# PV of two slots after fourteen rounds, in the MLP's groups of an attention and MLP block

## The chip, the cores and the metric

The kernel runs on one core of a Trainium2 chip. The metric is the device time of one execution in microseconds, and the numbers of a profile come from one profiled execution on that core. Engines are named as in the profile: PE is TensorE (PEld its weight loads), DVE is VectorE, ACT is ScalarE, POOL is GpSimd, SP issues the DMAs.

## The reference

The input x is 2048 tokens of 512 numbers. Its layer norm feeds two branches, which meet at the end:

```python
xn = _layernorm(x, axis=-1)
# A: qkv = xn @ wqkv; 32 heads of 16 numbers each
scores = jnp.einsum("bhqd,bhkd->bhqk", q, k) * (Dh ** -0.5)
p = _softmax(scores, axis=-1)
o = jnp.einsum("bhqk,bhkd->bhqd", p, v)
s = o.transpose(...).reshape(B, S, D) @ wo
# B: F = 1792
h = jnp.einsum("bsd,df->bsf", xn, w1) + b1
h = jnp.where(h > 0, h, 0) ** 2
g = _silu(jnp.einsum("bsf,fd->bsd", h, w2) + b2)
return x + s * g
```

Attention is over all 2048 x 2048 pairs of every head, so scores, exponentials and the product with v (PV) are the bulk of branch A. Branch B is a dense MLP.

## The kernel before

**Slots.** Attention is cut into 32 units (four heads by 512 queries), and each unit into 16 slots (128 keys each), 512 slots in all. A slot has four score matmuls (`exp_mm`, L1125: 128 keys by 512 queries, one for each head, contraction over 64 rows of the array), four exponentials on ACT (L1132) and, two slots later, four PV matmuls (`pv_mm`, L362), one for each head. A PV matmul uses all 128 rows and 32 of the columns of the array, so the four of a slot run side by side. The program has four of them in a slot; the profile lists each as two instructions, a first and a second pass.

**Maxima.** The softmax's shift is taken from the scores themselves, 24 slots ahead (`LEAD`): `max_mm` (L289) makes 128 queries by 512 keys of scores in a PSUM bank, and DVE reduces the bank to its row maxima (L296), four in each slot. When a unit's maxima are complete, `shift` transposes them on PE (L326) into a bank of the same pool, DVE splits them (L328, L329), `keep` writes them to DRAM (L335) and `back` brings them into the rows of the queries' tiles (L355). Steps put off with `later` (these two among them) run at the `begin` of the slot that is so many ahead.

**Banks.** PSUM's eight banks are given out as follows: three for scores that ACT reads (`pe`), three for scores that DVE reduces (`pm`), one for the MLP's sums (`pd`), one for PV's accumulation (`pv`; after a unit's sixteenth slot `evac`, L372, copies it out on ACT). Each pool hands its banks out in turn.

**Lanes and rounds.** Score, max and MLP matmuls contract over 64 rows, so that two of them run at once, one in each half (lane) of the array's rows. The program emits them in pairs, one in each lane; the text calls such a pair a round. All matmuls stand in one queue of PE, in the order in which the code emits them (the schedule is written by hand for all engines).

**Groups of the MLP.** `dense` yields the MLP's work. From the second of eight token chunks on (256 tokens each) most of it comes as blocks of four slots, which `long_slots` (L1207) runs: two halves, in each of which one lane has the MLP's twelve units (`D`) and the other has most of the scores. A half is written in two parts:

```python
for part, (mine, theirs) in enumerate((("D" * 10, "msmsmsmsms"), ("DDss", "mmsm"))):
```

`m` is a max matmul, `s` a score matmul. The ten rounds of the first part have five `m` and five `s` in the lane beside the MLP; the four of the second part have three `m` and three `s`. After each part stand `max_end` (DMAs of coming tiles), `shift_due` (a `shift` that is due) and PV of one slot: in a half's first part the slot two before the part's slot `st`, and so in its second. With PV between, a group is ten rounds, PV, four rounds, PV, ten rounds, PV, four rounds, PV.

There are two kinds of groups. In `first_pair` (w1, L508 and on) a unit is two matmuls of 256 columns, the sums go through a relu on ACT (L533), emitted in the second half's second part after its second round; chunks 1 to 7 have seven such groups each, 49 in all. In `second` (w2) a unit is one matmul of 512 columns; chunks 1 to 6 have six such groups each and chunk 7 has three, 39 in all. So there are 88 groups, or 176 halves. Other slots of the MLP (`slot`) have four `m`, four `s` and PV each.

**Tiles of exponentials.** `exp_mm` takes its output tile from a ring `pt`: 14 tiles, 17 from the second chunk on, when three staging tiles (`ex`) join, and 14 again at the end of the MLP. `oldest_first` turns the ring so that its oldest tile comes first whenever its length changes.

Of the kernel before, what the change touches and what calls it, by code (L numbers as in the profile page):

```python
# [8 lines left out]
F32 = mybir.dt.float32  # L9
# [7 lines left out]
P = 128  # L17
# [10 lines left out]
LEAD = 24  # L28
# [3 lines left out]
NPT = 14  # L32
# [7 lines left out]
def kernel(  # L40
# [55 lines left out]
    with ExitStack() as ph:  # L96
# [5 lines left out]
        pv = ph.enter_context(tc.tile_pool(name="pv", bufs=1, space=PSUM))  # L102

        rot = {}
        turn = {"ka": 0, "qm": 0, "qe": 0, "pt": 0}

        def ring(name):
            t = rot[name][turn[name] % len(rot[name])]
            turn[name] += 1
            return t  # L110

        def oldest_first(name):
            n = turn[name] % len(rot[name])
            rot[name] = rot[name][n:] + rot[name][:n]
            turn[name] = 0

        def make_ring(name, pool, numbers, width):
            rot.setdefault(name, []).extend(
# [201 lines left out]
        def shift_due(g):  # L320
            if late and late[0][0] <= g:
                shift(late.pop(0)[1])
# [91 lines left out]
        def mlp_tasks(mp):  # L414
# [3 lines left out]
            ex = mp.enter_context(tc.tile_pool(name="ex", bufs=1))  # L418
# [123 lines left out]
            def second(c, tt):  # L542
                hT = state["hT"]
                ps = pd.tile([P, D], F32, name="pd_t")
                u = up.tile([P, D], F32, name="u")
                th = rs[tt].rearrange("p a b -> p (a b)")
                ts_ = slice(tt * P, (tt + 1) * P)

                if c == 0 and tt == 0:
                    for k in range(5, FO):  # L550
                        later(k - 4, lambda k=k: load_w2(k, 2))

                def post():
                    nc.scalar.activation(u, ps, AF.Copy)  # L554
                    nc.gpsimd.tensor_tensor(u, u, b2_t, op=ALU.add)  # L555
                    later(2, gate)

                def gate():

                    nc.scalar.activation(th, u, AF.Tanh, scale=0.5)  # L560
                    nc.gpsimd.tensor_scalar(th, th, 0.5, 0.5, op0=ALU.mult, op1=ALU.add)
                    nc.gpsimd.tensor_tensor(u, u, th, op=ALU.mult)
                    t0 = c * CW + tt * P
                    later(4, lambda: nc.sync.dma_start(g_d[t0 : t0 + P, :], u))

                mms = terms3(ps, [
                    (lambda a, q, fo=fo: hT[q, a, fo, ts_], lambda b, q, fo=fo: w2t[q, b, fo])
                    for fo in range(FO)
                ])
                if c == 0:  # L570
                    yield from halves(mms, (6,) * 7, post, 1)
                    return
                if c == NCK - 1 and tt:

                    for i, task in enumerate(halves(mms, (6,) * 7, post, 1)):
                        if i == 4:
                            oldest_first("pt")
                            rot["pt"][:] = [t for t in rot["pt"] if all(t is not x for x in rot["ex"])]
                        yield task
                    return  # L580

                if tt:
                    yield from halves(mms[:6], (6,), None, 1)
                    mms = mms[6:]
                for k in range(0, 36, 12):
                    yield from block(mms[k : k + 12], 1, post if tt and k == 24 else None)
                if not tt:
                    yield from halves(mms[36:], (6,), post, 1)
# [10 lines left out]
                yield [], None  # L599
            for c in range(NCK):  # L600
                if c == 1:

                    oldest_first("pt")
                    rot["pt"][:0] = rot["ex"]
                if c == 0:
                    for fo in range(FO):
                        yield from first(c, fo)
                else:
                    for f in range(FO // 2):
                        yield from first_pair(c, f)  # L610
                if c + 1 < NCK:
                    load_xc(c + 1)
                    state["part"] = 0
                    for k in range(8):
                        later(13 + k, load_part)
                else:
                    m1.close()
                    wo_setup()
                for tt in range(CW // P):
                    yield from second(c, tt)  # L620
# [246 lines left out]
        st = right(ln, "wq_st", 1)  # L867
# [217 lines left out]
        for g in range(LEAD):  # L1085
            shift_due(g)
            for j in range(2):
                max_mm(g, j)
            pump(8)
            for j in range(2):  # L1090
                max_mm(g, j)
            pump(8)
            max_end(g)
            if g == 0:
                raw_r = [load_w("wv", 3 * P, ((D + P, 3 * P),))]
            if g == 3:
                for ko in range(KO):
                    split_w(wr_t, ko, slice(3 * P, 6 * P), raw_r[0][:, ko])
                ln.close()
                pools["v"] = ph.enter_context(tc.tile_pool(name="vp", bufs=1))  # L1100
            if g == 12:
                s1.close()
                ep = ph.enter_context(tc.tile_pool(name="ep", bufs=1))
                rot["pt"] = [ep.tile([P, 512], F32, name=f"pt{i}") for i in range(NPT)]
                pools["n"] = ph.enter_context(tc.tile_pool(name="np", bufs=1))
            if g == 16:
                load_v(0)
                nc.sync.dma_start(b1_t, b1.rearrange("(fo p) -> p fo", p=P), allow_slow_non_contiguous=True)
                nc.sync.dma_start(b2_t, b2[None, :].to_broadcast([P, D]))
            if g % 2 and g < 16:  # L1110
                c, i = divmod(g // 2, 2)
                nc.sync.dma_start(
                    xn_d[i, :, :, c * 512 : (c + 1) * 512], xTs[c][:, i].bitcast(F32)
                )
        first.close()

        def exp_mm(st, j, pts, spare):
            u, kb = divmod(st, 16)
            qd = u // 4
            b = 64 * (j % 2)  # L1120
            if spare:
                se = pm.tile([P, 512], F32, name="pm_t")
            else:
                se = pe.tile([P, 512], F32, name="se")
            nc.tensor.matmul(  # L1125
                se, kas[qd, j // 2][b : b + 64, kb * P : (kb + 1) * P],
                qes[u][j // 2][b : b + 64, :],
                start=True, stop=True,
            )
            pts[j] = ring("pt")  # L1130
            assert all(t is not pts[j] for d in pts_all.values() if d is not pts for t in d.values()), (st, j)
            return nc.scalar.activation(pts[j], se, AF.Exp, scale=0.25)  # L1132

        pos = {}
# [1 line left out]
        def pv_step(st, pts):  # L1136
            u, kb = divmod(st, 16)
            if kb == 0:
                pos[0] = pv.tile([P, 512], F32, name="po")
            pv_mm(pos[0], u // 4, kb, pts)  # L1140
            if kb == NT - 1:
                if u < NU - 2:
                    evac(pos[0], u)
                elif u == NU - 2:
                    unit_inner(pos[0])
                else:
                    unit_final(pos[0])
# [19 lines left out]
                yield from wo_last(c)  # L1167

        pts = {}
        pts_all = pts  # L1170

        def slot(st, mms, post, fill=0):
            g = st + LEAD
# [33 lines left out]
        def long_slots(st0, units, post):  # L1207
# [11 lines left out]
            for h in range(2):  # L1219
                own, other = units[h], 1 - h  # L1220
                for part, (mine, theirs) in enumerate((("D" * 10, "msmsmsmsms"), ("DDss", "mmsm"))):
                    st = st0 + 2 * h + part
                    if st > st0:
                        begin(st)
                    for i, ops in enumerate(zip(mine, theirs)):
                        for lane in (h, other) if part else (other, h):
                            o = ops[0] if lane == h else ops[1]
                            if o == "D":
                                own.pop(0)()
                            elif o == "m":  # L1230
                                max_mm(g0, lane)
                            else:
                                use = s(lane)
                                if part and lane == h and i == 2:
                                    last_use[0] = use
                        if part and h and i == 1 and post is not None:
                            post()
                    max_end(st + LEAD)
                    shift_due(st + 1 + LEAD)
                    pv_step(st - 2, pts.pop(st - 2))  # L1240
            if post is not None:
                last_use[0] = None
            assert not todo[0] and not todo[1] and not units[0] and not units[1]
# [82 lines left out]
```

## Time and profile before

| | us |
|---|---|
| median of two runs | 1686.23 |
| the two runs | 1684.71, 1687.75 |
| span of the profiled execution | 1684.0 |
| PE busy | 1655.3 |
| DVE busy | 1349.0 |
| ACT busy | 1192.2 |
| POOL busy | 525.5 |

The span is from the first to the last instruction of the one profiled execution; it lies 0.7 below the faster of the two runs and 2.2 below their median, and that execution's own time is not listed apart from its span. In a row of the timeline stand the start and the length in microseconds, then engine, line, operation, output and inputs, shapes, and how many instructions the row merges; a bracket tells how long the engine was idle before and what ended that. Matmuls are pipelined, so their records overlap: the time from one start to the next tells more than a record's length.

### The profile page before, as it was taken

What the parts mean: (1) busy time and instruction counts of PE and PEld (TensorE: products, weight loads), DVE (VectorE), ACT (ScalarE), POOL (GpSimd) and SP (SyncE); (2) the same over time, 40 slices, a digit from 0 to 9 for tenths busy, and PEclk for the clock granted to TensorE, in tenths of its full rate; (3) what the DMA queues carried; (4) which work ended last, traced back from release to release, by engine and by line L of the source; (5) the groups of instructions that cost most, each with busy time, mean ns of one, the idle gap of its engine ahead of it and who ended that gap; (6) DMA issues with size and microseconds to landing.
All of it is one profiled execution on the core that took longest, in us unless ns stands there. A gap on an engine that the chain in (4) does not pass through costs nothing.

```text
span 1684.0 us, 35391 instructions
## 1 busy us (share of the span) xinstructions
PE 1655.3 (98%) x13296; PEld 941.3 (56%) x13296; DVE 1349.0 (80%) x2296; ACT 1192.2 (71%) x2354; POOL 525.5 (31%) x544
## 2 busy tenths in 40 slices
PE   6999999999999999999999999999999999999998
PEld 5766565556545655565466456545655565555533
DVE  6255688888888888888888888888888888887632
ACT  7211477777777777777777777777777777776685
POOL 4335566522212321231133113311221233134333
PEclk9999999999999999999999999999999999999998
DMA  8648566434333333433333334323433352157444
GB/s 282 177 144 268 165 204 186 117 83 141 90 90 92 116 83 99 100 105 78 103 117 85 85 93 142 95 65 105 137 81 83 82 151 57 44 169 228 140 125 134
DMA packets 156723, 208.00 MB, mean 124 GB/s; under 512 B 51272, under 2 KB 71240, under 8 KB 155016
## 3 DMA queue, kind: packets, MB, share of 16 engines
q1 hardware_dynamic: 156552, 205.74, 42.2%
q8 instruction: 105, 1.72, 0.4%
q14 instruction: 66, 0.54, 0.1%
HBM read 149.30 MB, written 56.09 MB: 122 GB/s over the span
## 4 chain that ended last, share of the span: by engine, by line
PE 88%; issue 4%; DMA 3%; POOL 2%; SPq 1%; DVE 1%; ACT 0%; POOLq 0%; ACTq 0%
PE po L362 27%; PE pm_t L289 17%; PE pd_t L236 16%; PE se L1125 12%; PE pd_t L204 6%; PE se L916 5%; PE se L947 3%; POOL ts L740 1%; POOL ts L741 1%; DMA oc<-on_d 0%; PE pm_t L816 0%; PE pm_t L326 0%; DMA xt<-in_A_x_dram 0%; DMA xc<-xn_d 0%; DMA hl<-r_d 0%
## 5 line engine op out<-in xcount | busy, mean ns | idle before, releaser
L296 DVE TENSOR_REDUCE mx<-pm_t 128x1 f32<-128x512 f32 x2048 | 1275.2, 684 | 233.0 <-PE pm_t L289 139.7
L1132 ACT ACTIVATE pt<-se 128x512 f32<-128x512 f32 x1730 | 902.9, 611 | 254.7 <-PE se L1125 221.6
L289 PE MATMUL pm_t<-ka,qm 64*128 64x512 f32 x2048 | 797.1, 423 | 3.9 <-DVE mx L296 3.7
L1125 PE MATMUL se<-qe,ka 64*128 64x512 f32 x2000 | 685.9, 402 | 0.0
L362 PE MATMUL po<-pt,v 128*32 128x512 f32 x3556 | 544.3, 604 | 0.0
L289 PEld LDWEIGHTS pm_t<-ka,qm 64*128 64x128 f32 x2048 | 352.8, 184 | 279.5 <-DVE mx L296 252.2
L1125 PEld LDWEIGHTS se<-qe,ka 64*128 64x128 f32 x2000 | 339.5, 184 | 21.3 <-issue 5.5
L236 PEld LDWEIGHTS pd_t<-xc,w1s 64*128 64x128 f32 x2352 | 292.1, 187 | 82.3 <-issue 82.2
L236 PE MATMUL pd_t<-xc,w1s 64*128 64x256 f32 x2352 | 332.2, 288 | 0.0
L236 PE MATMUL pd_t<-w2t,hT 64*128 64x512 f32 x936 | 259.9, 410 | 0.0
L236 PEld LDWEIGHTS pd_t<-w2t,hT 64*128 64x128 f32 x936 | 156.0, 184 | 71.2 <-issue 65.4
L362 PE MATMUL po<-ex,v 128*32 128x512 f32 x540 | 192.3, 605 | 0.0
L1132 ACT ACTIVATE ex<-se 128x512 f32<-128x512 f32 x270 | 147.5, 614 | 36.6 <-PE se L1125 31.6
L536 POOL TENSOR_TENSOR r<-r 128x512 f32<-128x512 f32 x49 | 50.9, 1040 | 331.3 <-ACT r L533 331.3
L362 PEld LDWEIGHTS po<-pt,v 128*32 128x32 f32 x3556 | 79.9, 108 | 132.3 <-issue 111.6
L555 POOL TENSOR_TENSOR u<-u,b_t 128x512 f32<-128x512 f32 x16 | 20.5, 1284 | 307.5 <-ACT u L554 307.5
L204 PE MATMUL pd_t<-w2t,hT 64*128 64x512 f32 x408 | 105.6, 391 | 0.0
L400 POOL TENSOR_TENSOR ot<-ot,hl 128x512 f32<-128x512 f32 x31 | 39.8, 1284 | 185.5 <-DMA hl<-r_d 134.8
L204 PE MATMUL pd_t<-wot,oc 64*128 64x512 f32 x336 | 90.4, 405 | 2.4 <-DVE m L316 0.8
L204 PEld LDWEIGHTS pd_t<-wot,oc 64*128 64x128 f32 x336 | 58.6, 184 | 49.1 <-DVE mx L296 12.5
L204 PEld LDWEIGHTS pd_t<-w2t,hT 64*128 64x128 f32 x408 | 72.6, 184 | 8.9
L533 ACT ACTIVATE r<-pd_t,b_t 128x256 f32<-128x256 f32 x98 | 41.1, 470 | 50.1 <-PE pd_t L236 50.1
(111 smaller groups left out, 1110.4 us busy)
## 6 DMA issues: line engine op xcount, KB each, us to landing
w1s<-w_d SPq DMA_DIRECT2D x196, 256.0 KB
qm<-q_d SPq DMA_DIRECT2D x384, 32.0 KB
qe<-q_d SPq DMA_DIRECT2D x384, 32.0 KB
ka<-k_d SPq DMA_DIRECT2D x96, 128.0 KB
xn_d<-xT SPq DMA_DIRECT2D x8, 1024.0 KB
k_d<-hl SPq DMA_DIRECT2D x32, 256.0 KB
q_d<-hl SPq DMA_DIRECT2D x32, 256.0 KB
xc<-xn_d SPq DMA_DIRECT2D x16, 512.0 KB
```

The lines of the kernel that those rows point to most:

```text
L204: mm = nc.tensor.matmul(out_, lh(r), rh(r), start=first_ and lane == 0, stop=last_ and lane == 1, skip_group_check=True,)
L236: mm = nc.tensor.matmul(out_, lh(r), rh(r), start=first_ and lane == 0, stop=last_ and lane == 1, skip_group_check=True,)
L289: nc.tensor.matmul(ps, qms[u][p][64 * j : 64 * j + 64, qb * P : (qb + 1) * P], kas[qd, p][64 * j : 64 * j + 64, kc * 512 : (kc + 1) * 512] ...
L296: return nc.vector.tensor_reduce(mxs[u][:, c, kc : kc + 1], ps, axis=AX.X, op=ALU.max)
L362: nc.tensor.matmul(po[32 * j : 32 * j + 32, :], vs[qd][:, (4 * kb + j) * VW : (4 * kb + j) * VW + 32], pts[j], start=(kb == 0), stop=(kb = ...
L400: nc.gpsimd.tensor_tensor(ot, ot, hl[:, 1].bitcast(F32), op=ALU.mult)
L533: nc.scalar.activation(r[:, i], ps[:, i * CW : (i + 1) * CW], AF.Relu, bias=b1_t[:, fo : fo + 1])
L536: nc.gpsimd.tensor_tensor(r, r, r, op=ALU.mult)
L916: nc.tensor.matmul(out_, lh(slice(0, P)), rh(slice(0, P)), start=first_, stop=last_)
L947: nc.tensor.matmul(out_, lh(slice(0, P)), rh(slice(0, P)), start=first_, stop=last_)
L1125: nc.tensor.matmul(se, kas[qd, j // 2][b : b + 64, kb * P : (kb + 1) * P], qes[u][j // 2][b : b + 64, :], start=True, stop=True,)
L1132: return nc.scalar.activation(pts[j], se, AF.Exp, scale=0.25)
```

## The change

In `long_slots` a half is no longer cut by PV after its first part. After all fourteen rounds comes `shift_due`, and then PV of two slots in one go. `begin` and `max_end` stay between the parts, and the order of `m`, `s` and `D` stays.

The exponentials' tiles no longer come from a ring but from a list of free tiles: `exp_mm` takes the first, and `pv_step` appends a slot's four tiles when its PV is emitted. The three staging tiles are put at the head of the list at the second chunk, and are kept out of it from the end of the MLP on (`gone_pt`).

```diff
@@ exp_mm
-            pts[j] = ring("pt")
+            pts[j] = free_pt.pop(0)
@@ pv_step
             pv_mm(pos[0], u // 4, kb, pts)
+            free_pt.extend(t for _, t in sorted(pts.items()) if all(t is not x for x in gone_pt))
@@ mlp_tasks
-                    oldest_first("pt")
-                    rot["pt"][:0] = rot["ex"]
+                    free_pt[:0] = rot["ex"]
@@ long_slots
                     max_end(st + LEAD)
-                    shift_due(st + 1 + LEAD)
-                    pv_step(st - 2, pts.pop(st - 2))
+                shift_due(st + 1 + LEAD)
+                for kb in (st - 3, st - 2):
+                    pv_step(kb, pts.pop(kb))
```

Lines move up by two to four in the changed kernel: the max matmul is L287 there, its reduction L294, the score matmul L1121, PV L360, the transpose L324.

More of the change, by code (lines that the diff above doesn't have):

```diff
@@ L104 @@
         rot = {}
-        turn = {"ka": 0, "qm": 0, "qe": 0, "pt": 0}
+        turn = {"ka": 0, "qm": 0, "qe": 0}
         def ring(name):
@@ L110, in ring @@
             return t
[L112 to L115, printed above, removed]
+        free_pt = []
+        gone_pt = []
         def make_ring(name, pool, numbers, width):
@@ L576, in second @@
                         if i == 4:
-                            oldest_first("pt")
-                            rot["pt"][:] = [t for t in rot["pt"] if all(t is not x for x in rot["ex"])]
+                            gone_pt.extend(rot["ex"])
+                            free_pt[:] = [t for t in free_pt if all(t is not x for x in gone_pt)]
                         yield task
@@ L601, in mlp_tasks @@
                 if c == 1:
-                    oldest_first("pt")
-                    rot["pt"][:0] = rot["ex"]
+                    free_pt[:0] = rot["ex"]
                 if c == 0:
@@ L1103 @@
                 ep = ph.enter_context(tc.tile_pool(name="ep", bufs=1))
-                rot["pt"] = [ep.tile([P, 512], F32, name=f"pt{i}") for i in range(NPT)]
+                free_pt.extend(ep.tile([P, 512], F32, name=f"pt{i}") for i in range(NPT))
                 pools["n"] = ph.enter_context(tc.tile_pool(name="np", bufs=1))
@@ L1129, in exp_mm @@
             )
-            pts[j] = ring("pt")
-            assert all(t is not pts[j] for d in pts_all.values() if d is not pts for t in d.values()), (st, j)
+            pts[j] = free_pt.pop(0)
             return nc.scalar.activation(pts[j], se, AF.Exp, scale=0.25)
@@ L1169 @@
         pts = {}
-        pts_all = pts
         def slot(st, mms, post, fill=0):
```

## Prediction

> **What bounds the kernel now.** I read the page first, then busy times by stretch, then the timeline of single groups, engine by engine.
>
> ```profile
> span 1684.0 us, 35391 instructions
> ...
> PE 1655.3 (98%) x13296; PEld 941.3 (56%) x13296; DVE 1349.0 (80%) x2296; ACT 1192.2 (71%) x2354; POOL 525.5 (31%) x544
> ```
>
> PE is busy for 98% of the span: PE is the bound, and DVE at 80% is the next. The change touches only groups of the MLP, so I look at what a half of such a group does there: the first row below is a half of the first kind (w1), the second a half of the second kind (w2).
>
> ```profile
> 907.55:913.26 5.71, 5.71 (x61) 3.54 (x57) 4.97 (x9) 4.30 (x10) 1.68 (x3) 1.00 0.30 52
> 924.65:930.30 5.65, 5.65 (x48) 2.79 (x44) 4.97 (x9) 4.58 (x11) 2.59 (x3) 1.00 0.75 234
> ```
>
> The columns are length, then PE, PEld, DVE, ACT and POOL busy, then the clock, granted in full (1.00). PE does not rest in either. DVE has 4.97 of 5.71 in a half: 0.7 us is all the slack it has. So I need to know where in a half the slack lies. The timeline of PE in the first of these halves (an L289 row is an `m`, an L1125 row an `s`, L362 is PV), then DVE and ACT in the same half:
>
> ```profile
> 907.55 0.50 PE L289 MATMUL pm_t<-ka,qm 64*128 64x512 f32 x1
> ...
> 909.53 0.40 PE L289 MATMUL pm_t<-ka,qm 64*128 64x512 f32 x1
> ...
> 909.77 0.39 PE L1125 MATMUL se<-qe,ka 64*128 64x512 f32 x1
> ...
> 910.14 1.06 PE L362 MATMUL po<-pt,v 128*32 128x512 f32 x8
> ...
> 911.14 0.50 PE L289 MATMUL pm_t<-ka,qm 64*128 64x512 f32 x1
> ...
> 911.48 0.39 PE L289 MATMUL pm_t<-ka,qm 64*128 64x512 f32 x1
> ...
> 911.94 0.39 PE L289 MATMUL pm_t<-ka,qm 64*128 64x512 f32 x1
> ...
> 912.26 1.06 PE L362 MATMUL po<-pt,v 128*32 128x512 f32 x8
> 913.26 0.50 PE L289 MATMUL pm_t<-ka,qm 64*128 64x512 f32 x1
> ```
>
> ```profile
> 908.09 3.08 DVE L296 TENSOR_REDUCE mx<-pm_t 128x1 f32<-128x512 f32 x5 [0.21 <-PE pm_t L289]
> 911.71 1.89 DVE L296 TENSOR_REDUCE mx<-pm_t 128x1 f32<-128x512 f32 x3 [0.54 <-PE pd_t L236]
> ```
>
> ```profile
> 908.39 2.56 ACT L1132 ACTIVATE pt<-se 128x512 f32<-128x512 f32 x5 [0.39 <-PE pd_t L236]
> 911.97 0.84 ACT L533 ACTIVATE r<-pd_t,b_t 128x256 f32<-128x256 f32 x2 [1.03 <-PE pd_t L236]
> ```
>
> Rounds follow each other by 0.24 (909.53 to 909.77). Five `m` come in the first part; DVE takes their five banks in one run of 3.08, one each 0.60 ((3.08 - 1.89) / 2), and gets through it just as PV ends. The PV that is taken out here is the pause in which DVE catches up.
>
> **The change part by part.**
>
> *PV taken out between the parts: a gain.* The tenth round starts at 909.77 and the eleventh at 911.14: 1.37 in place of 0.24. The round after it comes 0.34 later (911.48), again not 0.24. So one PV costs 1.13 + 0.10 = 1.23. It is not removed but put behind another PV, and there it needs no change between row lanes and column tiles. At the end of the kernel PVs follow each other directly:
>
> ```profile
> 1666.30 1.04 PE L362 MATMUL po<-pt,v 128*32 128x512 f32 x8
> ```
>
> Two passes of four take 1.04 from the first start to the last end there. A pass after another lasts 0.59, and the four start within 0.02, so one pass follows the other by 1.04 - 0.59 - 0.02 = 0.43; the 0.59 stands in the tile's own row:
>
> ```profile
> L362 PE MATMUL po<-pt,v x3556: 592/593/618, 195.4 to 1668.3; 128*32 128x512 f32 x198
> ```
>
> A PV behind a PV costs 0.86, so each half gains 1.23 - 0.86 = 0.37. With 176 halves (49 + 39 groups of two) that is 65 us, if nothing takes its place.
>
> The Trainium skill, "TensorEngine Tiling (Array Packing)", Tiling Modes, says that changing the tiling mode drains the TensorE. The trace agrees, at 0.37 for a change there and back. By that rule alone the sum would end at 1684 - 65 = 1619.
>
> *The eighth max of a half: a wait that is new.* Without PV, the fourteenth round, which has the half's eighth `m`, would start 2.22 + 4 x 0.235 = 3.16 after the half's first `m`. But `pm` has three banks, so the eighth `m` needs the bank of the fifth, and DVE has to be through with five reductions. The first starts 0.54 after its matmul (907.55 to 908.09), five take 3.08: 3.62. DVE reads these five back to back already now, so nothing brings that end forward. How a PE that stood still for a bank goes on is seen in the few slots without MLP work:
>
> ```profile
> 1486.91 0.49 PE L289 MATMUL pm_t<-ka,qm 64*128 64x512 f32 x1 [0.32 <-DVE mx L296]
> ...
> 1487.33 1.07 PE L362 MATMUL po<-pt,v 128*32 128x512 f32 x8
> ...
> 1489.61 0.50 PE L289 MATMUL pm_t<-ka,qm 64*128 64x512 f32 x1 [0.31 <-DVE mx L296]
> ...
> 1490.04 1.07 PE L362 MATMUL po<-pt,v 128*32 128x512 f32 x8
> ```
>
> ```profile
> 1486.16 2.48 DVE L296 TENSOR_REDUCE mx<-pm_t 128x1 f32<-128x512 f32 x4 [0.38 <-PE se L1125]
> ```
>
> The first of those four reductions ends at 1486.16 + 0.69 = 1486.85, and the matmul starts 0.06 later. From it to PV are 0.42 and 0.43, where a half without a wait has 0.32 (911.94 to 912.26): after a wait the weights are still to be loaded. So the eighth `m` starts at 3.62 + 0.06 = 3.68, PV at 3.68 + 0.42 = 4.10. The first PV takes 1.00 to the next matmul (912.26 to 913.26), the second 0.86 more, so the next half starts at 5.96. The seventh `m` waits too (for the fourth reduction, 3.02 + 0.06 = 3.08), but its two rounds more, 0.34 + 0.23, end at 3.65 and are covered by the eighth's wait.
>
> A half now takes 5.71 or 5.65, and then 5.96 in both kinds, since nothing of the MLP's rounds is in that chain any more: 98 halves x 0.25 = 24.5, and 78 x 0.31 = 24.2. Together 49 us lost, with the gain of 65 already in it. DVE then finishes eight reductions at 0.54 + 3.08 + 3 x 0.60 = 5.42 and sits idle until 5.96 + 0.54: the two PVs in a row are longer than what three banks hold for it.
>
> The Trainium skill, "TensorEngine Tiling (Array Packing)", PSUM Bottleneck, warns that tiling speeds up the TensorE but not the emptying of PSUM, which may become the bottleneck. It gives no price, but it speaks against this change, and the reductions' rows bear it out at 0.60 each. By it the kernel ends at 1733 instead of 1619 before the rest is counted.
>
> *The eighth score of a half: a wait that costs nothing.* ACT's three banks tie the eighth `s` to the fifth exponential: 908.39 - 907.55 = 0.84, plus 2.56, is 3.40, plus 0.06 is 3.46. It hides behind the eighth `m` at 3.68. Without that cover it would still hold the half to 3.46 + 0.42 + 1.86 = 5.74. The relus of the first kind (0.84) stand behind the fifth exponential on ACT, so they delay only the last three, whose banks are asked for after PV.
>
> *`shift` after the second part: a small loss.* One of 16 slots has it, 22 of the 352.
>
> ```profile
> 901.64 0.50 PE L289 MATMUL pm_t<-ka,qm 64*128 64x512 f32 x1
> ...
> 904.22 0.28 PE L326 MATMUL pm_t<-ident,m 128*16 128x128 f32 x1
> 904.43 1.07 PE L362 MATMUL po<-pt,v 128*32 128x512 f32 x8
> ```
>
> That half takes 5.91 (901.64 to 907.55), 0.20 more than its neighbour. Moved, the transpose needs the bank of the sixth `m`, free at 3.62 + 0.60 + 0.06 = 4.28; PV follows 0.21 to 0.31 later, at 4.49 to 4.59 instead of 4.10. That is 0.39 to 0.49 in place of 0.20: 22 x 0.24 = 5 us. Its DVE work (two short operations) falls into DVE's idle time. `keep` and `back` go to SP one slot later, in the tenth and eleventh of a unit's slots, and their rows are read from slot 16 of that count: over four slots, some 11 us, lie between, against 0.6 us for an issue of `keep`:
>
> ```profile
> L335 SPq DMA_DIRECT2D sh_d<-sh x64: 608/618/755, 159.5 to 1615.9; - x64
> ```
>
> *The free list, `begin`, `evac`: nothing.* Sixteen tiles of exponentials are held at most, of 17. In the second half an exponential writes a tile that PV has just read, but its score matmul stands behind that PV in PE's queue, so the wait for it covers the other. With fewer than 16 tiles it would not fit at all. `begin` issues the same DMAs at the same places. `evac` has fourteen rounds instead of ten before PV asks for its bank, and the MLP's sums have one PV more for their relu.
>
> Sum, against the profiled span: 1684 + 49 + 5 = 1738. The median of the two runs lies 2 above that span: 1740.
>
> **The rivals.**
>
> *It pays off (faster).* If the eighth `m` finds its bank free, a half takes 5.34, and the time is 1686 - 65 = 1621. It decides at a wait of zero, so at five reductions within 3.16 - 0.54 - 0.06 = 2.56; the row says 3.08, and also ACT's 3.46 would have to go. It is also what the page's rule on drains would give by itself. Only a bank count that I read wrong brings it. Chance 7%.
>
> *The wait costs less (within 2%).* If PE has the weights of the eighth `m` loaded by the time of its bank, because that last wait is short (3.65 to 3.68), PV follows 0.32 later and a half takes 5.86: 98 x 0.15 + 78 x 0.21 = 31, with no more for `shift`: 1686 + 31 = 1717. Should only ACT's wait hold (5.74), it is 98 x 0.03 + 78 x 0.09 = 10: 1696. Against it: in both rows with a wait PV came at 0.42 and later. Chance 18%.
>
> *It costs more.* If each of the two waits adds its reload of 0.10 (the seventh's isn't covered), a half takes 6.06: 98 x 0.35 + 78 x 0.41 = 66, and with 5 for `shift` 1757. Chance 15%, in the slow class with the forecast.
>
> **How the numbers follow.** Forecast 60%, costs more 15%, costs less 18%, pays off 7%. The time is the forecast's, 1740. The range goes from 1716 (the cheap wait) to 1757; outside lie the 7%, the ACT case and a little above, less than 2 in 10. Two per cent, about what a measurement of this kernel can tell from no change, is 34 us: 1720. Faster by over 2%: 0.07. Within 2%: 0.18. Slower by over 2%: 0.75.
>
> **What would show it.** In the changed kernel, halves of both kinds repeat every 5.96; the eighth max starts 3.68 after the first, right after the end of a reduction, and PV 0.42 after it, lasting 1.9 in one row of 16. DVE has eight reductions in one run of about 4.9 and then 1.0 idle, in place of 0.5 and 0.2. Weight loads of the max matmul idle longer for DVE. The forecast is wrong if the eighth `m` starts near 3.2, if halves stay near 5.3, or if the two kinds of halves differ as they do now.

## The result, and the profile after

| | before | after |
|---|---|---|
| median of two runs, us | 1686.23 | 1736.57 |
| span of the profiled execution, us | 1684.0 | 1736.0 |

The changed kernel takes 1.030 of the time (95% interval 1.027 to 1.033): 50 us more, where 54 were forecast (1740).

First the page of the kernel after: busy times, and the chain that ended last.

```profile
PE 1703.8 (98%) x13296; PEld 1023.9 (59%) x13296; DVE 1332.8 (77%) x2296; ACT 1196.5 (69%) x2354; POOL 525.2 (30%) x544
...
PE 85%; DVE 6%; issue 3%; DMA 2%; POOL 2%; SPq 1%; ACT 0%; POOLq 0%; DVEq 0%; ACTq 0%
PE po L360 25%; PE pm_t L287 21%; PE pd_t L234 12%; PE se L1121 11%; PE pd_t L202 6%; DVE mx L294 5%; PE se L912 5%; PE se L943 3%; DMA xt<-in_A_x_dram 1%; DMA g<-g_d 1%; POOL ts L737 1%; POOL ts L736 1%; PE pm_t L812 0%; PE pm_t L324 0%; SPq L132 0%
```

The chain of the kernel before, from its page:

```profile
PE 88%; issue 4%; DMA 3%; POOL 2%; SPq 1%; DVE 1%; ACT 0%; POOLq 0%; ACTq 0%
PE po L362 27%; PE pm_t L289 17%; PE pd_t L236 16%; PE se L1125 12%; PE pd_t L204 6%; PE se L916 5%; PE se L947 3%; POOL ts L740 1%; POOL ts L741 1%; DMA oc<-on_d 0%; PE pm_t L816 0%; PE pm_t L326 0%; DMA xt<-in_A_x_dram 0%; DMA xc<-xn_d 0%; DMA hl<-r_d 0%
```

PE is still busy for 98%, so by busy shares nothing seems to wait. The chain tells otherwise: the reductions (mx L294) now have 5% of it, where the list before doesn't name them. Next, the timeline of PE in one half of the first kind (L287 is an `m`, L360 PV), and DVE's:

```profile
940.77 0.49 PE L287 MATMUL pm_t<-ka,qm 64*128 64x512 f32 x1
...
943.25 0.50 PE L287 MATMUL pm_t<-ka,qm 64*128 64x512 f32 x1
...
943.84 0.50 PE L287 MATMUL pm_t<-ka,qm 64*128 64x512 f32 x1
...
944.44 0.49 PE L287 MATMUL pm_t<-ka,qm 64*128 64x512 f32 x1
944.86 0.62 PE L360 MATMUL po<-ex,v 128*32 128x512 f32 x1
...
946.72 0.49 PE L287 MATMUL pm_t<-ka,qm 64*128 64x512 f32 x1
```

```profile
941.30 4.88 DVE L294 TENSOR_REDUCE mx<-pm_t 128x1 f32<-128x512 f32 x8 [1.08 <-PE pd_t L234]
947.25 3.08 DVE L294 TENSOR_REDUCE mx<-pm_t 128x1 f32<-128x512 f32 x5 [1.07 <-PE pm_t L287]
```

The last three `m` of the half (sixth to eighth) start 2.48, 3.07 and 3.67 after the first, 0.60 apart: DVE's pace, not PE's 0.24. PV follows the eighth by 0.42, and the next half starts at 5.95. DVE has its eight reductions in one run and then 1.07 idle. The second row below is a half of the second kind (w2); the columns are length, then PE, PEld, DVE, ACT and POOL busy, then the clock.

```profile
940.77:946.72 5.95, 5.95 (x62) 4.00 (x58) 4.88 (x8) 4.13 (x8) 1.29 (x1) 1.00 0.05 9
970.00:975.95 5.95, 5.95 (x52) 3.18 (x44) 4.95 (x9) 4.13 (x8) 0.00 (x1) 1.00 0.27 66
```

Both kinds take 5.95, where they had 5.71 and 5.65. PE counts as busy in all of it: a matmul's record is 0.39 to 0.50 long and overlaps the next, so a wait of 0.35 (from the sixth `m` to the seventh 0.59 pass in place of 0.24) disappears in it. The views of waits say as little. Two rows of the lists of waits, before and after (weight loads, what they waited for, us in total, times, the longest):

```profile
PEld pm_t L289 <- DVE mx L296: 252.2, 352, 1.6
```

```profile
PEld pm_t L287 <- DVE mx L294: 255.0, 436, 1.4
```

### The profile page after: what moved, and what is told of

Read it like the earlier page. It is cut to its first block, busy times and chain, and to the rows that moved or that the text cites. A ratio compares the mean times of both kernels' runs of the same rounds, so it can differ in the third digit from the quotient of the medians.

```text
span 1736.0 us, 35235 instructions
## 1 busy us (share of the span) xinstructions
PE 1703.8 (98%) x13296; PEld 1023.9 (59%) x13296; DVE 1332.8 (77%) x2296; ACT 1196.5 (69%) x2354; POOL 525.2 (30%) x544
## 4 chain that ended last, share of the span: by engine, by line
PE 85%; DVE 6%; issue 3%; DMA 2%; POOL 2%; SPq 1%; ACT 0%; POOLq 0%; DVEq 0%; ACTq 0%
PE po L360 25%; PE pm_t L287 21%; PE pd_t L234 12%; PE se L1121 11%; PE pd_t L202 6%; DVE mx L294 5%; PE se L912 5%; PE se L943 3%; DMA xt<-in_A_x_dram 1%; DMA g<-g_d 1%; POOL ts L737 1%; POOL ts L736 1%; PE pm_t L812 0%; PE pm_t L324 0%; SPq L132 0%
## 5 line engine op out<-in xcount | busy, mean ns | idle before, releaser
L294 DVE TENSOR_REDUCE mx<-pm_t 128x1 f32<-128x512 f32 x2048 | 1259.2, 683 | 299.1 <-PE pm_t L287 195.9
L287 PE MATMUL pm_t<-ka,qm 64*128 64x512 f32 x2048 | 862.1, 441 | 3.9 <-DVE mx L294 3.6
L1121 PE MATMUL se<-qe,ka 64*128 64x512 f32 x2000 | 718.1, 418 | 0.0
L287 PEld LDWEIGHTS pm_t<-ka,qm 64*128 64x128 f32 x2048 | 365.2, 184 | 348.6 <-DVE mx L294 255.0
L360 PE MATMUL po<-pt,v 128*32 128x512 f32 x3544 | 508.2, 600 | 0.0
L1121 PEld LDWEIGHTS se<-qe,ka 64*128 64x128 f32 x2000 | 353.1, 185 | 18.1 <-issue 5.5
L234 PE MATMUL pd_t<-xc,w1s 64*128 64x256 f32 x2352 | 306.5, 284 | 0.0
L234 PE MATMUL pd_t<-w2t,hT 64*128 64x512 f32 x936 | 239.3, 401 | 0.0
L360 PE MATMUL po<-ex,v 128*32 128x512 f32 x552 | 223.0, 599 | 0.0
L1127 ACT ACTIVATE ex<-se 128x512 f32<-128x512 f32 x276 | 164.5, 605 | 51.2 <-PE pd_t L234 34.0
L360 PEld LDWEIGHTS po<-pt,v 128*32 128x32 f32 x3544 | 97.4, 108 | 164.6 <-issue 152.9
L202 PE MATMUL pd_t<-w2t,hT 64*128 64x512 f32 x408 | 105.8, 392 | 0.0
L81 POOL TENSOR_TENSOR hT<-r,hT 128x512 fp32r<-128x512 f32 x56 | 72.2, 1288 | 4.7
```

The source lines that it names most:

```text
L81: (lo or nc.gpsimd).tensor_tensor(dst[1], raw, dst[0].bitcast(F32), op=ALU.subtract)
L202: mm = nc.tensor.matmul(out_, lh(r), rh(r), start=first_ and lane == 0, stop=last_ and lane == 1, skip_group_check=True,)
L234: mm = nc.tensor.matmul(out_, lh(r), rh(r), start=first_ and lane == 0, stop=last_ and lane == 1, skip_group_check=True,)
L287: nc.tensor.matmul(ps, qms[u][p][64 * j : 64 * j + 64, qb * P : (qb + 1) * P], kas[qd, p][64 * j : 64 * j + 64, kc * 512 : (kc + 1) * 512] ...
L294: return nc.vector.tensor_reduce(mxs[u][:, c, kc : kc + 1], ps, axis=AX.X, op=ALU.max)
L360: nc.tensor.matmul(po[32 * j : 32 * j + 32, :], vs[qd][:, (4 * kb + j) * VW : (4 * kb + j) * VW + 32], pts[j], start=(kb == 0), stop=(kb = ...
```

## The experiments

The theory under test is the bank theory: a half is lengthened by its eighth max, which waits until DVE has emptied the bank of the fifth. Rivals are the list of free tiles, ACT's banks, the two PVs in a row, and DVE's total load.

| run | median, us | against the kernel before (95% interval) |
|---|---|---|
| e1_list_only | 1685.96 | 0.9999 (0.9989 to 1.0008) |
| e2_thin_max | 1682.24 | 0.9972 (0.9962 to 0.9981) |
| e3_thin_exp | 1736.28 | 1.0300 (1.0282 to 1.0319) |
| e4_thin_both | 1626.81 | 0.9655 (0.9636 to 0.9675) |
| e5_before_thin_both | 1684.92 | 0.9993 (0.9984 to 1.0003) |
| e6_second_half | 1709.57 | 1.0142 (1.0124 to 1.0159) |
| e7_two_banks | 1941.43 | one run |
| e8_thin_max_scores_first | 1646.09 | 0.9757 (0.9742 to 0.9771) |
| e9_scores_first | 1778.68 | 1.0541 (1.0523 to 1.0558) |

**The list alone.**

```diff
                     max_end(st + LEAD)
-                shift_due(st + 1 + LEAD)
-                for kb in (st - 3, st - 2):
-                    pv_step(kb, pts.pop(kb))
+                    shift_due(st + 1 + LEAD)
+                    pv_step(st - 2, pts.pop(st - 2))
```

> The changed kernel with PV back where it was (ten rounds, PV of one slot, four rounds, PV of one slot, shift after either part); only the list of free tiles stays. Bank theory (the loss is the eighth max waiting for one of three banks that DVE reduces): the list costs nothing, halves take 5.70 and 5.65 as before, 1686 us in all, within 3 us of the kernel before. List theory (tiles taken in another order make exponentials wait for PV): a good part of the 50 us stays, 1700 to 1736.

1685.96: the list of free tiles costs nothing. All of the 50 us belongs to the place of PV and of `shift`, which moved with it.

**Thin reductions.** `thin[0]` is set inside `long_slots` alone.

```diff
-                mxs[u][:, c, kc : kc + 1], ps, axis=AX.X, op=ALU.max
+                mxs[u][:, c, kc : kc + 1], ps[:, : 128 if thin[0] else 512], axis=AX.X, op=ALU.max
```

> The changed kernel, but in the MLP's groups DVE reduces only 128 of a bank's 512 columns, so the row maxima are those of a quarter of the keys there. Matmuls, banks, waits and order stay. Bank theory: the eighth max finds its bank free; what holds the half then is ACT's three banks, with the eighth score at 3.46, so both kinds of halves take 5.71 to 5.74 instead of 5.95: 1736 - 176 x 0.23 = 1696 (1690 to 1703). PV theory (two PVs in a row, or what follows them, cost the time by themselves) and list theory: no change, 1736.

1682.24: with cheaper reductions, and every matmul and PV as in the changed kernel, the loss is gone and 4 us with it. PV and list theories fall. A half of it on PE, then ACT in the same half (L1129 is the exponential):

```profile
906.58 0.50 PE L289 MATMUL pm_t<-ka,qm 64*128 64x512 f32 x1
...
909.47 0.98 PE L1123 MATMUL se<-qe,ka 64*128 64x512 f32 x3
909.96 0.49 PE L289 MATMUL pm_t<-ka,qm 64*128 64x512 f32 x1
910.38 0.62 PE L362 MATMUL po<-pt,v 128*32 128x512 f32 x2
...
912.24 0.49 PE L289 MATMUL pm_t<-ka,qm 64*128 64x512 f32 x1
```

```profile
907.35 1.09 ACT L1129 ACTIVATE pt<-se 128x512 f32<-128x512 f32 x2 [1.65 <-PE pd_t L234]
908.32 0.60 ACT L1129 ACTIVATE ex<-se 128x512 f32<-128x512 f32 x1
908.80 1.11 ACT L1129 ACTIVATE pt<-se 128x512 f32<-128x512 f32 x2
```

The eighth max starts 3.38 after the first, not yet at 3.16. The fifth exponential ends at 908.80 + 1.11 = 909.91, and 0.05 later the fourteenth round goes on: the wait that the prediction called covered has become the one that decides. The half takes 5.66. Expected were 5.71 and more, and 1690 at least; ACT's first exponential started 0.77 after the half did (906.58 to 907.35), where I had used 0.84.

**Thin exponentials.**

```diff
-            return nc.scalar.activation(pts[j], se, AF.Exp, scale=0.25)
+            w = 128 if thin[0] else 512
+            return nc.scalar.activation(pts[j][:, :w], se[:, :w], AF.Exp, scale=0.25)
```

> The changed kernel, but in the MLP's groups ACT makes exponentials of only 128 of a bank's 512 columns; the rest of each tile keeps older values, and PV reads the whole tile. Bank theory: ACT's wait is covered by DVE's, so nothing moves: halves 5.95, 1736 (within 3). ACT theory (the eighth score's wait for ACT is what lengthens a half): halves fall to 5.3 to 5.7, 1620 to 1700.

1736.28, the changed kernel's time to 0.3 us. ACT's wait alone is worth nothing while DVE's is longer.

**Both thin, in the changed kernel and in the one before.** The two edits together.

> The changed kernel with both: in the MLP's groups DVE reduces and ACT makes exponentials of 128 of 512 columns, so maxima come from a quarter of the keys and three quarters of each tile of exponentials are older values. Bank theory: no bank is waited for any longer, and the saving of 0.37 in each half shows: halves of 5.33 to 5.40 in place of 5.95, 1621 to 1633 us. PV theory (PV pairs cost more than two PVs apart, whoever reads the banks): 1736, or at least not under 1686.

> The kernel before, with the reductions and exponentials of the MLP's groups cut to 128 of 512 columns as in the run before this one (the same quarter of the keys in the maxima, the same older values in the tiles). Bank theory: before the change no half waits for DVE or ACT, PE's own work and its changes of mode fill it, so nothing moves: halves 5.70 and 5.65, 1686 us (within 4). The difference to the changed kernel with both cut is then the changes of mode alone, 176 x 0.37 = 65 us. If the kernel before did wait for DVE or ACT somewhere in its halves: faster by 10 us or more.

1626.81 and 1684.92. The kernel before gains next to nothing from reductions and exponentials of a quarter of the length (ratio 0.9993): PE fills its halves. One of its halves (e5) still takes 5.70:

```profile
884.82 0.50 PE L291 MATMUL pm_t<-ka,qm 64*128 64x512 f32 x1
...
890.52 0.50 PE L291 MATMUL pm_t<-ka,qm 64*128 64x512 f32 x1
```

The changed one gains 110 us. The difference of the two runs, 58 us or 0.33 for each of 176 halves, is what PV between the parts costs more than PV behind a PV, where no bank is waited for; the prediction had 0.37 and 65. That it is the change of tiling mode that costs it fits the rows, but no run separates it from weight loads that come late there. A half of e4 on PE:

```profile
884.82 0.49 PE L289 MATMUL pm_t<-ka,qm 64*128 64x512 f32 x1
...
887.92 0.39 PE L289 MATMUL pm_t<-ka,qm 64*128 64x512 f32 x1
888.04 0.39 PE L1123 MATMUL se<-qe,ka 64*128 64x512 f32 x1
888.36 0.62 PE L362 MATMUL po<-ex,v 128*32 128x512 f32 x1
...
890.21 0.49 PE L289 MATMUL pm_t<-ka,qm 64*128 64x512 f32 x1
```

The eighth max comes 3.10 after the first, without a wait, but the last score of the other lane 0.12 later, and PV 0.32 after that. That lane has the MLP's pairs of 256 columns, and each of its rounds takes 0.01 longer; after twelve the lanes are 0.12 apart, where a PV after the tenth round used to bring them together again. So a half of the first kind takes 5.39, not 5.34: 98 x 0.05 = 5 of the 7 us by which the 65 were too large.

**One half of two.** PV of two slots only where `h` is 1; the first half is cut as before.

> The changed kernel, with PV of two slots in one go only at the end of a group's second half; the first half is cut as before (shift too stands there as before). Bank theory: each half goes by its own three banks, so the first takes 5.70 or 5.65 and the second 5.95: 49 x 0.25 + 39 x 0.30 = 24 us over the kernel before, 1710 (1705 to 1714). Backlog theory (DVE falls behind over several halves and the loss comes of its total load, 80% of the span): DVE has slack over a whole group, so half the merges cost little or even gain: 1654 to 1690.

1709.57: 23 us more than the kernel before, near half of the 50. In its second half on PE:

```profile
885.13 0.50 PE L287 MATMUL pm_t<-ka,qm 64*128 64x512 f32 x1
...
888.81 0.50 PE L287 MATMUL pm_t<-ka,qm 64*128 64x512 f32 x1
889.24 0.62 PE L360 MATMUL po<-ex,v 128*32 128x512 f32 x1
...
891.09 0.50 PE L287 MATMUL pm_t<-ka,qm 64*128 64x512 f32 x1
```

The eighth max stands at 3.68 and the half takes 5.96, right behind a half that is cut as before. The trace has 88 such second halves, and all of them take 5.94 to 5.96. Nothing builds up from half to half; the backlog theory falls. DVE's average load over a group isn't what counts, but what three banks hold across one gap.

**One bank less.** `bufs=4` for `pe` and `bufs=2` for `pm`.

> The changed kernel with two banks for maxima and four for scores, in the whole kernel. Bank theory: the eighth max of a half waits for the sixth reduction, 0.60 later than now, and earlier ones wait too: halves of 6.55 to 6.75 in place of 5.95, and 1840 to 1910 in all with the other slots' own waits. If it is DVE's pace alone that counts, and not how many banks stand between: halves stay at 5.95, and 1736.

```profile
886.50 0.49 PE L287 MATMUL pm_t<-ka,qm 64*128 64x512 f32 x1
...
893.22 0.50 PE L287 MATMUL pm_t<-ka,qm 64*128 64x512 f32 x1
```

A half takes 6.72, inside the expected 6.55 to 6.75: the number of banks counts, while a reduction takes as long as before (median 0.69, after 0.68). The fourth bank for scores came in by the same edit; it gives the scores more room, not less. The total of 1941 lies over the expected 1910: I had put too little on the slots outside the groups, which share the two banks. Added up from the starts in the two traces, the groups take 139 us longer than in the changed kernel, and the other slots 62.

**Scores first.** The edit of both runs, with and without thin reductions:

```diff
-                for part, (mine, theirs) in enumerate((("D" * 10, "msmsmsmsms"), ("DDss", "mmsm"))):
+                for part, (mine, theirs) in enumerate((("D" * 10, "smsmsmsmsm"), ("DDss", "smmm"))):
```

> The changed kernel with full reductions and the same exchange of s and m (smsmsmsmsm and smmm). Nothing is added or left out, only the half's first max comes a round (0.34) later, and the last two stand next to each other. Bank theory: the whole run of reductions starts later by the round, five end at 3.86 to 3.92, and halves grow from 5.95 to 6.15 to 6.27: 1770 to 1792 us. If the loss came of the two PVs, of ACT or of the free list, the exchange would do nothing or help: 1736 or less.

1778.68, inside the expected range. DVE's run in it, after an idle time of 1.31:

```profile
880.21 4.88 DVE L294 TENSOR_REDUCE mx<-pm_t 128x1 f32<-128x512 f32 x8 [1.31 <-PE pm_t L287]
886.39 3.08 DVE L294 TENSOR_REDUCE mx<-pm_t 128x1 f32<-128x512 f32 x5 [1.31 <-PE pd_t L234]
```

One run starts 6.18 after the other, 0.23 more than with maxima first (5.95). No work was added: the time is made by when DVE's run begins.

> The changed kernel with reductions of 128 of 512 columns in the MLP's groups (maxima of a quarter of the keys there), and s and m changed places in the lane beside the MLP: smsmsmsmsm and smmm in place of msmsmsmsms and mmsm. Bank theory: with DVE out of the way the eighth score's wait for ACT holds a half at 5.66; with scores one round earlier ACT's first exponential starts 0.54 after the half does instead of 0.77 to 0.84, five end at 3.10, and the eighth score, due at 3.16, hardly waits. Halves of 5.34 to 5.48, 1627 to 1652 us, under both kernels. If something else than ACT's banks holds the half at 5.66: no change, 1682.

1646.09, under both kernels and inside the expected range. ACT in one of its halves, and that half's last max:

```profile
883.38 2.56 ACT L1129 ACTIVATE pt<-se 128x512 f32<-128x512 f32 x5 [0.68 <-PE pd_t L234]
```

```profile
886.00 0.50 PE L289 MATMUL pm_t<-ka,qm 64*128 64x512 f32 x1
```

Five exponentials end at 885.94, and the round with the eighth score, which has the last max too, goes on 0.06 later. So ACT's banks seem to hold the half a little still: the halves' median is 5.46, between the 5.66 of e2 and the 5.39 of e4. This version isn't a drop-in for the kernel: its softmax shift is the largest of a quarter of the keys in the groups. Softmax doesn't depend on the shift, but the exponential of a key outside the quarter whose score is far larger could overflow. With full reductions no run beat the kernel before.

## Why the prediction was right

Added up from the starts in the two traces, the 176 halves take 49.7 us longer after the change, of the 52.0 by which the spans differ; the rest lies ahead of the first PV. Of the 49.7, some 46 are the longer halves (49 forecast) and just under 4 the halves with `shift` (5 forecast).

*PV taken out between the parts, 65 us gained.* Right in kind, a little too large: 58 us where no bank is waited for (e4 against e5), mostly since the lanes drift apart over fourteen rounds, which I had left out. The error does no harm to the 1740: the half's 5.96 is built from DVE's run and two PVs, and the 65 enter only the rival that pays off.

*The eighth max's wait.* Right, step by step: eighth max at 3.67 (3.68 forecast), PV 0.42 after it (0.42), two PVs to the next half 1.86 (1.86), half 5.95 (5.96), the same in both kinds. That its cause is DVE's reductions and the number of banks is shown by e2, e7 and e9 from three sides. The reload after a wait decided between the forecast and the rival within 2%: with PV at 0.32 it would have been 1717. The list of weight loads bears the reload out: those of the eighth `m` start with it at 944.44 after the change, where before they start 0.23 ahead of it (911.71 for 911.94).

*The seventh max's wait is covered.* Right: it starts at 3.07, and the eighth 0.60 later, as DVE gives the banks free.

*The eighth score's wait is covered.* Right: e3 moves nothing, and e2 shows it as the next to decide. Its 3.46 was 0.08 late (3.38 in e2); behind the longer wait for DVE that changed nothing.

*`shift`, 5 us.* Right in kind, slightly too large. A half with it, on PE:

```profile
976.47 0.50 PE L287 MATMUL pm_t<-ka,qm 64*128 64x512 f32 x1
...
980.74 0.28 PE L324 MATMUL pm_t<-ident,m 128*16 128x128 f32 x1
980.95 1.50 PE L360 MATMUL po<-pt,v 128*32 128x512 f32 x12
```

The transpose stands at 4.27 (4.28 forecast) and PV 0.21 after it, at 4.48 against 4.09 in a half without. The loss over the old place is 0.39 - 0.20 = 0.19, the cheap end of what was worked out. The trace has 23 halves with it, not 22.

*The free list: nothing.* Right (e1).

*One sign was named wrongly.* I had said that weight loads of the max matmul would idle longer for DVE. They idle 255.0 in place of 252.2, and 223.7 even in e5, where the groups' reductions are a quarter as long and the halves take what they took before. The view that names DVE is the chain, but its share is no price either: the reductions have 1% of it in e6, which loses 23 us, and 30% in e9, which loses 92.

## What to carry to other kernels

Work that looks like a cost on the busiest engine can be the pause in which another engine empties its banks: before merging such pieces, write down when the bank is free that the last producer ahead of the gap needs (here the fifth reduction's end, 3.62), and when that producer would come (3.16). Slack of a second engine, 20% on average here, is worth something across a gap only as far as the banks between the two reach. And where records overlap, a wait doesn't show as idle time: compare starts, and read the chain.

## What was not expected of the hardware

An idle ACT didn't begin at one fixed time after its score matmul. In the halves shown it began 0.50 after it before (907.89 to 908.39) and 0.42 after it in the changed kernel, as this row of ACT and the one of PE below it tell; no run here says why.

```profile
941.53 1.57 ACT L1127 ACTIVATE pt<-se 128x512 f32<-128x512 f32 x3 [1.18 <-PE pd_t L234]
```

```profile
941.11 0.39 PE L1121 MATMUL se<-qe,ka 64*128 64x512 f32 x1
```
